# A two-layer state-space mix: preparing the per-kernel numbers once, in three widths, and a new order of the queues

## The chip, the cores and the metric

The program runs on one core of a Trainium2 chip. The metric is the device time of one execution in microseconds, given as the median of several executions. A core has a tensor engine (PE, whose weight loads are listed as PEld), a vector engine (DVE), a scalar engine for tables of functions (ACT), a general engine (POOL) and SP, which here only starts DMA transfers. Each engine works through its own queue in order and waits on semaphores for what others have to deliver.

## The reference

Two S4 layers with different parameters read the same input u (2048 steps, 512 channels). Each layer builds one long convolution kernel per channel from 128 complex modes, convolves and adds a skip; a gate mixes the two results.

```python
def layer(u, A_re, A_im, B_re, B_im, C_re, C_im, log_dt, Dskip):
    dt = jnp.exp(log_dt)[:, None]
    logdA = dt * (A_re + 1j * A_im)                     # 512 x 128
    dB = dt * (B_re + 1j * B_im)
    P = jnp.exp(logdA[:, :, None] * arange(L))          # 512 x 128 x 2048
    K = jnp.einsum("dn,dnl,dn->dl", C_re + 1j * C_im, P, dB).real
    y = irfft(rfft(pad(u)) * rfft(pad(K)))[:L]          # causal convolution
    return y + u * Dskip

g = sigmoid((u * gate_w).sum(-1, keepdims=True))
return g * layer_A(u) + (1 - g) * layer_B(u)
```

## The kernel before

The 512 channels are cut into 8 chunks of 64; a chunk has 128 kernels (64 channels of both layers), one row of 128 numbers per parameter and mode. All arithmetic is float32, with angles as 32-bit integers that wrap. The work of a chunk has these parts:

- **Preparation** (`prep`, `N` = 128 columns): from the parameter rows and dt 35 small instructions make five numbers per kernel and mode: `al` (decay times dt), `rho` (size of C times B times dt), and the integer angles `z64`, `wa`, `zh`. Five products are fixed on POOL and one on DVE, twelve more may go to either (`heng="any"`); the others are DVE operations, a reciprocal (line 432) among them, and five functions on ACT. Results and temporaries lie in rings of tiles of one chunk's width (`par_in`, `m1`, `m2`, `m`, `e`, `kr`, `al`, `rho`, `z64`, `wa`, `zh`), most with one buffer. dt is spread over the partitions once (`spread_dt`), stored in DRAM (`dtd`) and read back for each chunk (`load_dt`).
- **Seeds** (`seed`, `seed_angles`): 25 exponentials on ACT in a row (line 471) write powers of the decay into `ml` and `mh`; three POOL products write angles `sa` and multiply `rho` into `mh`.
- **Tables** (`tables`, eight per chunk, T = 0 to 63, 16 kernels each): POOL forms the angles `ang`; POOL or DVE forms the decays `mr` from `ml` (128x1024) and from `mh` (128x512); ACT makes sine, half-angle sine and square into PSUM (`s`, `sq`); four DVE operations (lines 514 to 519, shown as L297 and L307) multiply them into `ei` and `mr`, of which the last two are the L307 instructions that write `mr`. PE (line 529) sums over the modes into the kernel's samples, which ACT or DVE copies to `kt`; after every second table PE runs the first stage of the kernel's Fourier transform (`first`, L549) into `xa` or `xb`.
- **Convolution** (`conv`, eight steps per chunk, s = 0 to 63): PE finishes the transform (L631, `fw`), DVE multiplies with the spectrum of u (L635, `y`), PE runs the first inverse stage with the constants `vv` (L644, L645), a copy to `z` and a store to `zb` follow.
- **End** (`fin`): `zb` is read back as `f`, PE runs the last inverse stage with the gate matrix `gsi` (L673), and the result is stored.

Beside them `u_spectra` makes the spectra of u (L549, L572), which go to DRAM, and `gated` makes the gate matrix (L593). The constants `w2` and `vv` are loaded at the start.

`prep(n)` for the next chunk stands in the program at the first table of a chunk, so the preparation of chunks 1 to 7 is spread over the whole run. What is executed when is not the program's order: `ORDER`, a list of 2068 numbers, gives the order of all operations, and so each queue's; a `b` behind a number takes the second of two possible engines (DVE instead of POOL for products, DVE instead of ACT for copies). Helpers record the operations, so many have the same line in the profile: L297 is `tensor_tensor`, L302 `tensor_scalar`, L307 `scalar_tensor_tensor`, L310 ACT functions, L320 and L322 copies on ACT and DVE, L315 transfers.

Of the kernel before, what the change touches and what calls it, by code (L numbers as in the profile page):

```python
# [22 lines left out]
CH = 2 * DC  # L23
# [4 lines left out]
GROUPS = tuple((c,) for c in range(8))  # L28
# [50 lines left out]
1 0 3 89 93 250 23 24 25 249 26 27 28 41b 44b 30 31 46b 43 5 47 90 42 9 45 32 48 55 33 54 49 34 35 6 7 22 92 91b 97 50 2 51 94  # L79
17 14 29 52b 36 4 53 37 82 12 38 15 95b 13 39 64 101 56 65 96 66 20 57 98 58b 71b 61 67b 62b 68 59 63 40 70 75 60 251 76 100b  # L80
69 72 73 77 74b 79 99b 253 309 102 252b 254 16 8 322 83 103 104b 310 111 78 114 313 311b 324b 312b 84 85 325b 316 340 86 314
87 317 112 115b 275 315 113 123 323 129 116 318 80 326 120 338 319 327 329 81 124 117 339 328 125 330 133 341b 342 331 351 320
343 352 332 121 353b 118 333 321 119 344 122 345 255 278 277 276 280b 346 10 354 355 11 279 367 281 356 334b 347 348 335 88
257 256 358 368 357 349 369 359 282 336 360 371 105 382 361 106 350 258 107 337 370b 372 362 380 374 18 1501 373 108 381 375
363 126 383b 384 376 109 385 110 130 377 396 398 127 387 386 259 397 388 131 283 400 1494 389 409 1487 1495 401 399 390 137
1488 132 284 1502 290 402 364 285 128 261 260 291 286b 292b 378 287 289 298 293 295 365 288 274 296b 366b 466 299 425 379b 134
305b 304b 297 300 403 410 391 141 19 426 136b 21 135b 404 138 405 294 301b 392b 306 139 411b 413 393 302 307 412b 308b 406 303
429 140 428 416 394 395 427 142 417 414 468b 415 407 430 467 144 418 143 469 470 419 479 471 420 473 480 472 474 481 483 475
151 408 421b 484 431 476 482 422 152 495 486 153 496 487 148 423 497b 424 145 149 485 435 477 150 146b 499 498b 147 154 488
510 500 157 478b 489 155 1489 432 156 501 508 160 1490 158 490 524 159 502 262 433 1496 509 491 503 161 1491 162 437 504 512  # L90
511 1497 526 166 1492 515 513 163 1493 527 167 1503 516 168 505 492 434 1504 525 514 436 164 517 1510 1508 537 439 1509 493
165 528 506 494b 538 1515 518 529 1498 169 1516 539 531 1522 530 532 507b 519 553 1499 1511 541 1500 1505 554 533 1529 542 540
520b 1512 534 555 1506 544 543 1530 521 545 1523 1507 1513 447 556 546 557 1514 1517 558 448 535 566 1518 522 523 449b 1524
1536 536b 438 452 547 568 560 548 559 263 440 453b 450 561 567 1525 569 570 454 562 623 441 571 583 549b 264 442 265 573 1519
574 563 1531 1526 445 1520 270 572 1532 271 1527 443 582 1528 1538 451 1543 266 550 272 1521 1537 1550 575 1544 267 273 1551
564 551b 576 268 577 446 552 625b 1533 638b 565 444 578 269b 456 579 1539 462 455 1534 1535 461 580 463b 1557 457 581 464 1558
458b 465b 1545 459 654b 586 1540 585 1546 636 460 1571 1552 1572 1541 1547 584 1553 624 1542 1564 1559 1565 1548 626 627 1554
1560 1549 637 628 630 655 1578 1566 629 589 631 1561 1947 590 592 1567 591 640 639 1555 632 1573 1562 1556 594 1568 587 593
633 1579 652 596 1574 595 1563 1943 641 653 634 643 1585 642 1948 1586 644 1569 1592 602 665 645 1570 1575 635 1949 1950 666
656 646 647 657 603 598b 597 659 667 658 1944 660 1576 1580 683 661 648 1945 1946 669 649 1939 1581 1577 668 670 1606 173 662  # L100
1587 671 650 684 672 1935 1593 663 681 1582 682 1588 664 694 673 599 1599 1594 1600 604 651 685 605 688 674 600 1940 696 601
1583 1584 170 613 612 1941 686 1936 619b 614 606b 181 689 615 171 695 675 172 1937 174 609 687 1595 697 676 607 176 1607 177
690 710 698 711 175 691 677 699 678 610b 701 712 700 1589 702 680 679 723 703 714 692 724 704 1590 611 705 713b 715 1591 618b
1613 740 717 693 716 178 1614 718 706 1596 719 727 725 180 179b 728 720 707 729 620b 1597b 621 588 616 708 739 709b 182 622b
726b 721 780 209 1598 184b 743 730 608 617 183b 741 731 185 191 732 781 793 733 722 192b 186 794 734 784 193 782b 1942 188 187
1963 742 735 785 736 783b 795 189 787 190 197 737 1959 786 788 200 749b 738 796b 198 1601 789 811 199 1964 201 790 797 202 809
# [5 lines left out]
1655 754 886 763b 1656 766 764 745 1649 1961 865b 866 1638 1662 767b 896 768 887 937 888 1645 897 765 756 889 1650 878 890 950  # L112
1639b 760 755 1651 1640 891 757 1646 758 939b 1669 1652 1663 759 952b 769 892 1670 1647 1962 770 879 775b 1653 893 776b 777b
1654 771 778 772b 1952 779b 773 895 894b 899 900 1657 774 898 1956 1658 938 1953b 1664 1683 906b 941 1684 1979 1971 1659 940b
953b 942 968 903 1665 904 943 944 1671 1676 1957 1660 1666 1958 945 1677 908 1672 946 1661 951 1980 1954 901 947 954 969 966
948 1975 955 967 905 957 1678 956 958 1667 979 1981 959 970 1982 980 213 1673 1972 973 1690 981 1691 909 971 1679 1973 1974
907 960 1685 982 910 974 1674 949 918 972 961 917 1686 912 983 1976 911 975 1697 997 962 1967 1668 963 976 1977 1698 984 986
1675 1704 995 1705 985 916 919 977 1692 913 964 1008 978 987 1680 914 920b 915 988 996 965 1968 998 999 989 1693 1009 990 1681
1000 926 1682 1010 1002 1687 927 1969 991 1003 1001 933b 902 1699 921 928 923 1012 1011b 992 1688 1004 922 1024 1689 1694 1711
993 1005 929 994 1025 1700 1013 1006 932 1015 1695 1026 1014 1696 1706 1712 1016 1007 1701 1017 1028 934 924 1029 935 930 1018  # L120
1027 210 1702 1707 931 1030 1037 217 1031 211 1038 212 214 1032 925 1039b 1019 1041 221 1718 215 1040 1033 1725 1719 1020 1708
# [82 lines left out]
def ssm_mix(ctx: ExitStack, tc: tile.TileContext, a, out, dry=False):  # L204
# [180 lines left out]
    def prep(c, heng="any"):  # L385
# [18 lines left out]
        def W(n):  # L404
            return K(n)[:1]
# [360 lines left out]
```

## Time and profile before

| | before |
|---|---|
| median of 3 runs (lowest to highest) | 526.46 us (526.21 to 527.22) |
| the profiled execution, its span | 522.11 us, 520.3 us |
| mean granted PE clock | 0.950 |
| HBM read, written | 51.25 MB, 29.82 MB |

The profile is of one execution. Its page gives busy time by engine, a strip of 40 slices, the DMA queues, the chain of work that ended last, and groups of instructions as "line engine operation out<-in, shapes, count, busy us, mean ns of one, idle time before". Other views answer for a stretch of time, a tile or a wait. An instruction's duration includes time in which it stood at a resource that another engine held, and DVE's and ACT's instructions overlap a little with the next one of their queue.

### The profile page before, as it was taken

Reading aid. Unit: us, or ns where it says so; the run is one execution under the profiler, and the core shown is the slowest. Engines: PE = TensorE matmul, PEld = TensorE weight load, DVE = VectorE, ACT = ScalarE, POOL = GpSimd, SP = SyncE. Lnnn points to the kernel's source line nnn. Section 1 sums busy time; section 2 is a strip of 40 time slices with the busy share of each in tenths; the row PEclk is TensorE's granted clock in tenths of the full one; section 3 lists DMA queues with packets and bytes.
Section 4 is the critical chain, followed back from the end, with each engine's and each line's share of the span. In section 5 each row is a group of like instructions: output and inputs, shape, how many; then the busy total and the mean of one; then the engine's idle time right before and its main releaser. Section 6 shows DMA issues by size and latency. Waiting matters only on the chain.

```text
span 520.3 us, 24035 instructions
## 1 busy us (share of the span) xinstructions
PE 427.2 (82%) x10566; PEld 396.2 (76%) x10566; DVE 442.9 (85%) x585; ACT 386.5 (74%) x694; POOL 371.7 (71%) x352
## 2 busy tenths in 40 slices
PE   3949868888699776998789879799798779799964
PEld 3738757887698766988688868699787669699964
DVE  6798989999879999999699989999899979795520
ACT  3976998677867889999668888879977697792110
POOL 2797778895498778897488986797988589770000
PEclk9987979999999999999899997989999798999997
DMA  7954571560467535563485343455557466554476
GB/s 225 313 162 132 177 245 64 153 186 10 130 183 224 156 103 153 166 183 115 134 243 164 90 151 106 132 144 153 159 160 206 117 173 195 138 154 114 156 218 164
DMA packets 82520, 82.62 MB, mean 159 GB/s; under 512 B 5904, under 2 KB 68880, under 8 KB 82416
## 3 DMA queue, kind: packets, MB, share of 16 engines
q1 hardware_dynamic: 82272, 80.69, 52.2%
q8 instruction: 83, 1.36, 1.1%
q0 software_dynamic: 144, 0.39, 0.2%
q14 instruction: 21, 0.17, 0.1%
HBM read 51.25 MB, written 29.82 MB: 156 GB/s over the span
## 4 chain that ended last, share of the span: by engine, by line
PE 35%; DVE 22%; ACT 20%; issue 9%; DMA 8%; POOL 3%; SPq 2%; DVEq 0%; ACTq 0%; POOLq 0%
PE c L644 6%; PE fw L631 6%; PE c L645 6%; PE c L529 5%; DVE mr L307 5%; PE c L549 5%; DVE ei L297 4%; DVE mr L297 4%; ACT ml L471 3%; DVE y L635 3%; ACT mh L471 3%; PE c L673 3%; DMA f<-zb 2%; DMA u<-us 2%; ACT sq L310 2%
## 5 line engine op out<-in xcount | busy, mean ns | idle before, releaser
L307 DVE SCALAR_TENSOR_TENSOR mr<-sq,mr 128x1024 f32<-128x1024 f32 (+1 forms) x128 | 118.4, 947 | 7.0 <-ACT sq L310 7.0
L644 PE MATMUL c<-y,vv 128*128 128x128 f32 x512 | 104.0, 285 | 5.9 <-ACT z L320 2.6
L297 POOL TENSOR_TENSOR mr<-ml 128x1024 f32<-128x1024 f32 x47 | 94.3, 2006 | 11.6 <-PE c L529 8.3
L645 PE MATMUL c<-y,vv 128*128 128x128 f32 x512 | 100.9, 279 | 1.2 <-issue 1.2
L297 POOL TENSOR_TENSOR ang<-zh,cint 128x512 int32<-128x512 int32 x64 | 69.2, 1082 | 28.2 <-ACT sq L310 22.5
L644 PEld LDWEIGHTS c<-y,vv 128*128 128x128 f32 x512 | 79.6, 196 | 8.6 <-ACT z L320 2.8
L529 PE MATMUL c<-mr 128*32 128x64 f32 x2048 | 67.9, 229 | 16.7 <-DVE mr L307 8.3
L310 ACT ACTIVATE s<-ang 128x1024 f32<-128x1024 int32 x64 | 66.0, 1031 | 20.0 <-DVE ei L307 10.9
L635 DVE TENSOR_TENSOR y<-fw,u 128x1024 f32<-128x1024 f32 x57 | 69.4, 1217 | 13.4 <-PE fw L631 11.8
L297 DVE TENSOR_TENSOR ei<-s,mr 128x1024 f32<-128x1024 f32 x64 | 77.7, 1215 | 3.4 <-ACT s L310 1.6
L645 PEld LDWEIGHTS c<-y,vv 128*128 128x128 f32 x512 | 79.6, 196 | 0.8 <-issue 0.8
L320 ACT ACTIVATE z<-c 128x512 f32<-128x512 f32 x84 | 49.1, 590 | 41.0 <-PE c L645 35.8
L310 ACT ACTIVATE sq<-ang 128x1024 f32<-128x1024 f32 x64 | 65.8, 1029 | 17.6 <-DVE mr L307 16.7
L297 POOL TENSOR_TENSOR ang<-sa 128x512 int32<-128x512 int32 x64 | 70.7, 1105 | 0.4
L529 PE MATMUL c<-ei 128*32 128x64 f32 x2048 | 66.9, 226 | 2.3 <-issue 2.3
L529 PEld LDWEIGHTS c<-mr 128*32 128x32 f32 x2048 | 50.3, 114 | 24.0 <-issue 8.8
L310 ACT ACTIVATE ang<-ang 128x1024 f32<-128x1024 int32 x64 | 67.6, 1056 | 1.1
L529 PEld LDWEIGHTS c<-ei 128*32 128x32 f32 x2048 | 52.4, 115 | 2.6 <-issue 2.6
L297 POOL TENSOR_TENSOR mr<-mh 128x512 f32<-128x512 f32 x45 | 51.5, 1146 | 0.0
L549 PE MATMUL c<-small,kt 64*64 64x64 f32 x2048 | 43.0, 229 | 10.1 <-ACT kt L320 5.3
L549 PEld LDWEIGHTS c<-small,kt 64*64 64x64 f32 x2048 | 37.1, 141 | 15.5 <-ACT kt L320 6.2
L307 DVE SCALAR_TENSOR_TENSOR ei<-s,mr 128x512 f32<-128x512 f32 x64 | 43.4, 679 | 0.0
(104 smaller groups left out, 828.8 us busy)
## 6 DMA issues: line engine op xcount, KB each, us to landing
zb<-z SPq DMA_DIRECT2D x64, 256.0 KB, 3.0
u<-us SPq DMA_DIRECT2D x114, 128.0 KB, 3.6
f<-zb SPq DMA_DIRECT2D x28, 512.0 KB, 5.5
us<-z SPq DMA_DIRECT2D x32, 256.0 KB, 2.5
uin<-in_uk_dram SPq DMA_DIRECT2D x16, 256.0 KB, 4.3
f<-in_ut_dram SPq DMA_DIRECT2D x8, 512.0 KB, 5.3
out_dram<-o SPq DMA_DIRECT2D x29, 128.0 KB, 3.6
par_in<-in_par_dram SPq DMA_DIRECT2D x8, 384.0 KB, 3.5
```

The costliest lines, as they stand in the source:

```text
L297: op(engs, 0, lambda e: (dve if e == "dve" else pool).tensor_tensor(out=out(), in0=in0(), in1=in1(), op=o), reads, writes, port=port)
L307: lambda _: dve.scalar_tensor_tensor(out=out(), in0=in0(), scalar=s, in1=in1(), op0=o0, op1=o1), reads, writes, port=port)
L310: op("act", c_act(n), lambda _: act.activation(out=out(), in_=in_(), func=func, **{k: v() if callable(v) else v for k, v in kw.items()}), ...
L320: act.activation(out=o(), in_=i(), func=AF.Copy)
L471: act.activation(out=t(*tile)[:, ks, j], in_=t("al", n)[:, w, ks], func=AF.Exp, scale=float(l))
L529: pe.matmul(ps[32 * j:32 * j + 32, o, 0:64], x[:, 4 * o + j, 64:96], x[:, 4 * o + j, 0:64], start=o + part == 0, stop=False, tile_position ...
L549: pe.matmul(t(*ps[h]).rearrange("p a b -> p (a b)")[64 * r:64 * r + 64, 64 * g:64 * g + 64], t(*x)[64 * h:64 * h + 64, g], t("small")[64 * ...
L631: pe.matmul(fv()[:, :, k], t("w2", j // 2)[:, 4 * (j % 2) + k], t(*x1)[:, 4 * j + k], start=True, stop=True)
L635: op("dve", 1134, lambda _: dve.tensor_tensor(out=t(*y).rearrange("p h s f d -> p h s (f d)"), in0=fv().rearrange("p s f d -> p s (f d)"). ...
L644: pe.matmul(t(*ps)[:, k], v[:, 64:192], t(*y)[:, 0, :, k], start=True, stop=False)
L645: pe.matmul(t(*ps)[:, k], v[:, 0:128], t(*y)[:, 1, :, k], start=False, stop=True)
L673: pe.matmul(t(*ps)[64 * r:64 * r + 64, i, 0:DC], t("gsi")[:, 4 * k + i, s, 64 * r:64 * r + 64], fv()[:, r, i, DC * s:DC * s + DC], start=s ...
```

## The change

The chunks are prepared in three groups: chunk 0 alone, chunks 1 to 3 together (384 columns) and chunks 4 to 7 together (512 columns), all in the head. `INS` (the six parameter rows and dt) of the two wide groups lie in the tile of `gsi`, and the temporaries in the four tiles of `vv`; both get their own contents afterwards, so the four `vv` loads and the gate copies stand behind the preparation. Chunk 0's rows lie in two `y` tiles. The five results of a wide group are stored to a DRAM tensor `prd` by five transfers; `load_par` reads one chunk's five rows (320 KB) into a ring `par` of two buffers, one chunk ahead. dt is no longer stored and read back.

The products of the wide groups stand for DVE first (`yna`), with `b` now naming POOL. No form of arithmetic changes. The order list is new throughout, 1901 numbers long. Counted from it:

| engine, operation | before | after |
|---|---|---|
| DVE instructions | 585 | 518 |
| DVE preparation | 152 | 76 (26 for chunk 0, 25 for each wide group) |
| POOL preparation | 88 | 14 |
| ACT preparation | 40 | 15 |
| `mr` products from `ml` on DVE, POOL | 17, 47 | 4, 60 |
| `mr` products from `mh` on DVE, POOL | 19, 45 | 7, 57 |
| `z`, `xa`, `xb` copies of 512 on ACT, DVE | 155, 37 | 129, 63 |
| `kt`, `o` copies of 256 on ACT, DVE | 78, 18 | 70, 26 |
| PE matrix products | the same | the same |

Up to table 4's last DVE operation the new order has all 50 DVE operations of the wide groups, 10 of their POOL operations, and three instead of two of the gate's row products. Behind it, DVE has 129 preparation operations fewer, 26 `mr` products become 7 (2 of 128x1024, 5 of 128x512, from 14 and 14 behind table 4), and copies to `z`, `xa`, `xb` on DVE rise from 31 to 54.

```diff
-GROUPS = tuple((c,) for c in range(8))
+GROUPS = ((0,), (1, 2, 3), (4, 5, 6, 7))
...
-    ring("par_in", 1, [128, GW, 7, CH])
-    for n in ("m1", "m2", "m", "e", "kr", "al", "rho"):
-        ring(n, 1, [128, GW, CH])
-    for n in ("z64", "wa"):
-        ring(n, 1, [128, GW, CH], I32)
-    ring("zh", 2, [128, GW, CH], I32)
+    ring("par", 2, [128, 5, CH], I32)
...
-        tiles["dtd",] = dp.tile([NCH, 128, CH], F32, name="dtd")
+        tiles["prd",] = dp.tile([NCH, 128, 5, CH], I32, name="prd")
...
     def load_params(n):
         for i, c in enumerate(GROUPS[n]):
...
+            if n:
+                dma(1100, lambda i=i: t("gsi").rearrange("p i s m -> p (i s m)").rearrange("p (r c k) -> p r c k", r=8, k=CH)[:, 0:6, i],
+                    lambda c=c: a["par"][c], (), [("row", r) for r in INS])
...
+    def load_par(c):
+        n = [c in g for g in GROUPS].index(True)
+        dma(350, lambda: t("par", c), lambda: t("prd")[c], [("prd", n, r) for r in OUTS], [("par", c)])
...
+    def place(n, name):
+        if n == 0:
...
+        w = CH * len(GROUPS[n])
+        if name in TEMPS:
+            k, i = divmod(TEMPS.index(name), 3)
+            return lambda: t("vv", k).rearrange("p f m -> p (f m)")[:, 512 * i:512 * i + w], w, ("row", name), []
+        i = 5 + n if name == "dt" else INS.index(name)
+        return lambda: t("gsi").rearrange("p i s m -> p (i s m)")[:, 512 * i:512 * i + w], w, \
...
+        def mul(o, x, y, kind=OP.mult):
+            r = rd(o, x, y)
+            tt("any" if n == 0 else "yna", N, V(o), V(x), V(y), kind, r, W(o), 2)
...
+        if n:
+            c0, w = GROUPS[n][0], len(GROUPS[n])
+            for i, r in enumerate(OUTS):
+                dma(90 * w, lambda i=i: t("prd")[c0:c0 + w, :, i].rearrange("c p k -> p c k"),
+                    lambda r=r: V(r, I32)().rearrange("p (c k) -> p c k", k=CH), K(r), [("prd", n, r)])
...
-    load_dt(1)
+    for n in (1, 2):
+        load_params(n)
+        prep(n)
+    for k in range(4):
+        load_w("vv", k, 192)
...
-            if c + 1 < NCH and where[c + 1][1] == 0:
-                n = where[c + 1][0]
-                if c:
-                    load_params(n)
-                    load_dt(n)
-                prep(n)
+            if c + 1 < NCH:
+                load_par(c + 1)
```

More of the change, by code (lines that the diff above doesn't have):

```diff
@@ L214, in ssm_mix @@
     NT = NCH * NG
-    GW = max(len(g) for g in GROUPS)
-    where = {c: (n, i) for n, cs in enumerate(GROUPS) for i, c in enumerate(cs)}
     NJ = F1 // 4
@@ L370, in spread_dt @@
            [("small",), ("dt",)], [key])
-        for h in range(0, n, 4):
-            m = min(4, n - h)
-            ps = ("c", "spread", lo, h)
+        for g, cs in enumerate(GROUPS):
+            if (g == 0) != (lo == 0):
+                continue
+            h, m, ps = cs[0] - lo, len(cs), ("c", "spread", g)
             op("pe", 214 * m, lambda _, h=h, m=m, ps=ps: pe.matmul(t(*ps)[:, 0:m], t("small")[:, 449:577], dg()[:, h:h + m],
-                                                                  start=True, stop=True), [key, ("small",)], [ps])
-            if lo == 0:
-                actv(CH, lambda: t("par_in", 0)[:, 0, 6], lambda ps=ps: t(*ps)[:, 0], AF.Copy, [ps, ("par_in", 0)], [("dt", 0)])
-            else:
-                actv(CH * m, lambda h=h, m=m: dg()[:, h:h + m], lambda ps=ps, m=m: t(*ps)[:, 0:m], AF.Copy,
-                     [ps], [key])
@@ L381, in spread_dt @@
-        if lo:
-            dma(1300, lambda: t("dtd")[lo:lo + n].rearrange("c p k -> p c k"), dg, [key], [("dtd",)])
-    def prep(c, heng="any"):
-        w = len(GROUPS[c])
-        N = w * CH
-        rows = ("a_re", "a_im", "c_re", "b_re", "c_im", "b_im", "dt")
-        px = ("par_in", c)
-        def V(n, d=None):
-            if n in rows:
-                v = lambda: t(*px)[:, 0:w, rows.index(n)]
-            else:
-                v = lambda: t(n, c)[:, 0:w]
+                                                              start=True, stop=True), [key, ("small",)], [ps])
@@ L397, in V, with prep @@
+    def prep(n):
+        N = place(n, "dt")[1]
+        new = set()
+        def V(name, d=None):
+            v = place(n, name)[0]
             return v if d is None else lambda: v().bitcast(d)
         def K(*names):
-            keys = [("dt", c) if n == "dt" else ("row", n, c) if n in rows else (n, c) for n in names]
-            return keys + [px] * any(n in rows for n in names)
-        quarter = lambda: t("small")[:, 577:578]
-        def W(n):
-            return K(n)[:1]
-        def mul(eng, o, x, y, kind=OP.mult):
-            tt(eng, N, V(o), V(x), V(y), kind, K(x, y, o) if o in rows else K(x, y), W(o), 2)
@@ L423, in prep, with W, rd @@
-        mul(heng, "m1", "c_re", "b_re")
-        mul("pool", "b_im", "b_im", "c_im", OP.add)
-        mul(heng, "m1", "m1", "m2", OP.subtract)
+            return [k for x in names for k in (place(n, x)[2], *place(n, x)[3])]
+        def W(name):
+            _, _, key, tile_ = place(n, name)
+            first = [k for k in tile_ if k not in new and k != ("y", "prep", 0)]
+            new.update(first)
+            return [key] + first
+        def rd(o, *names):
+            return K(*names) + [k for k in place(n, o)[3] if k in new or k == ("y", "prep", 0)]
@@ L430, in prep @@
         t2(s, ap, 1e-30, aq, OP.max, OP.add)
-        mul(heng, d, aq, ap, OP.subtract)
+        mul(d, aq, ap, OP.subtract)
         op("dve", 67 + 6.27 * N, lambda _: dve.reciprocal(out=V(s)(), in_=V(s)()), K(s), W(s))
-        mul(heng, d, d, s)
+        mul(d, d, s)
         f(d, d, AF.Arctan, table=9)
@@ L596, in gated @@
             op("pe", 3440, mm, [*fs, ("gate_w",)], [ps], table="full")
-            copy(512, lambda h=h: t("gsi")[:, 4 * h:4 * h + 4, 0], lambda ps=ps: t(*ps), [ps], [w])
+            copy(512, lambda h=h: t("gsi")[:, 4 * h:4 * h + 4, 0], lambda ps=ps: t(*ps), [ps],
+                 [w] + [("row", r) for r in INS] + [("row", "dt", n) for n in (1, 2)])
         ws = [("gsi", h) for h in range(4)]
@@ L691, in ssm_mix @@
         load_w("w2", k, 128)
-    load_params(1)
     load("dsk")
-    for k in range(4):
-        load_w("vv", k, 192)
     actv(1, lambda: t("dummy"), lambda: t("dummy"), AF.Exp, [("dummy",)], [("dummy",)], table=0)
```

205 lines of the change are left out of this document (105 added, 100 removed), and 35 rows, old and new, of the table ORDER.

## The prediction

> **What bounds the kernel now.** I read the page first: busy times and the chain that ended last.
>
> ```profile
> span 520.3 us, 24035 instructions
> ...
> PE 427.2 (82%) x10566; PEld 396.2 (76%) x10566; DVE 442.9 (85%) x585; ACT 386.5 (74%) x694; POOL 371.7 (71%) x352
> ...
> PE 35%; DVE 22%; ACT 20%; issue 9%; DMA 8%; POOL 3%; SPq 2%; DVEq 0%; ACTq 0%; POOLq 0%
> ```
>
> Nobody is full over the span: PE 82%, DVE 85%, ACT 74%, POOL 72%. The chain walks over PE, DVE and ACT in turn, so the kernel is a pipeline in which several engines are nearly full at once, and an average share decides nothing. I therefore cut the span at two places that mean the same in both orders. The instructions of line 307 that write mr come two to a table (128x1024, then 128x512); the tenth on DVE closes table 4 and ends at 55.7:
>
> ```profile
> 53.91 1.81 DVE L307 SCALAR_TENSOR_TENSOR mr<-sq,mr 128x1024 f32<-128x1024 f32 x2
> ```
>
> The other cut is 457, where table 60 is closed. The windows view over these stretches (busy us of each engine, with instruction counts):
>
> ```profile
> core 0: us, PE busy (x) PEld busy (x) DVE busy (x) ACT busy (x) POOL busy (x), PEclk, DMA share, GB/s
> 0.00:56.00 56.00, 38.74 (x740) 32.44 (x744) 44.79 (x76) 39.16 (x73) 38.25 (x48) 0.91 0.67 213
> 56.00:457.00 401.00, 337.52 (x8877) 314.66 (x8867) 369.11 (x478) 329.05 (x593) 323.48 (x296) 0.96 0.51 151
> 457.00:520.30 63.30, 50.97 (x967) 49.07 (x965) 29.02 (x33) 18.29 (x30) 9.93 (x10) 0.94 0.58 163
> ```
>
> The head is 56 us: DVE 80%, PE 69%. The middle is 401 us: DVE 92%, PE 84.2%, ACT 82%, POOL 81%. The tail has no per-kernel numbers in it and POOL nearly idle. So DVE leads the middle, but there is a second resource that DVE and POOL hold in common. The timeline by engine at 300 us:
>
> ```profile
> 299.38 3.67 POOL L297 TENSOR_TENSOR sa<-z,cint 128x1536 int32<-128x1536 int32 x1 [0.23 <-DVE z L302]
> 301.43 1.78 DVE L297 TENSOR_TENSOR rho<-rho,par_in 128x128 f32<-128x128 f32 x1
> ```
>
> A DVE product of 128 elements takes 1.78 us; it ends at 303.21, just behind POOL's 3.67 us one, which ends at 303.05. The same group by duration (min/median/max, ns) and a larger one:
>
> ```profile
> L297 DVE TENSOR_TENSOR rho<-rho,par_in x8: 281/418/2135, 19.3 to 423.5; 128x128 f32<-128x128 f32 x8
> ```
>
> ```profile
> L297 DVE TENSOR_TENSOR mr<-mh x19: 677/1293/2446, 26.9 to 428.5; 128x512 f32<-128x512 f32 x19
> ```
>
> The same instruction costs 281 or 2135 ns, 677 or 2446 ns. That is waiting on POOL, counted as DVE's busy time. The Trainium skill, "SBUF — State Buffer", section "SBUF: two separate sides", says that DVE and GpSimd share one pair of ports under an exclusive lock which the first to start keeps for its whole instruction; the two rows at 300 us agree.
>
> **The change part by part.** Counts are read off the two order lists, split at table 4 and priced by rows of before.
>
> *Wide preparation, into the head.* All seven later chunks are now prepared ahead of table 4, as groups of 384 and 512 elements. Per group DVE gets 17 two-input operations, 7 one-input ones and a reciprocal. Rows for the price:
>
> ```profile
> L297 DVE TENSOR_TENSOR ei<-s,mr 128x1024 f32<-128x1024 f32 x64 | 77.7, 1215 | 3.4 <-ACT s L310 1.6 <-PE c L533 1.0
> L307 DVE SCALAR_TENSOR_TENSOR ei<-s,mr 128x512 f32<-128x512 f32 x64 | 43.4, 679 | 0.0
> L432 DVE RECIPROCAL par_in<-par_in 128x128 f32<-128x128 f32 x8 | 7.5, 941 | 0.0
> L302 DVE TENSOR_SCALAR m<-par_in 128x128 int32<-128x128 f32 x8 | 1.8, 219 | 0.0
> ```
>
> Two-input: (1215−679)/512 = 1.047 ns an element, 143 fixed, so 545 ns for 384 and 679 for 512. One-input: (219−143)/128 = 0.59, so 371 and 447. Reciprocal: (941−143)/128 = 6.23, so 2.54 and 3.34 us. Group one: 17×0.545+7×0.371+2.54 = 14.4; group two: 17×0.679+7×0.447+3.34 = 18.0; together 32.4 us of DVE, if nothing holds the port. Also in the head DVE gains four chunk-0 products (4×0.281 = 1.1), three copies and two short dt copies (about 3.1) and loses four mr products and two small ones (−6.4). Sum: +30.2 us.
>
> *Moved work.* The new order gives most mr products to POOL and copies to DVE:
>
> ```profile
> L297 POOL TENSOR_TENSOR mr<-ml 128x1024 f32<-128x1024 f32 x47 | 94.3, 2006 | 11.6 <-PE c L529 8.3 <-issue 2.2 <-ACT ml L471 1.2
> L297 POOL TENSOR_TENSOR mr<-mh 128x512 f32<-128x512 f32 x45 | 51.5, 1146 | 0.0
> L297 DVE TENSOR_TENSOR mr<-mh 128x512 f32<-128x512 f32 x19 | 25.5, 1348 | 0.0
> L297 DVE TENSOR_TENSOR mr<-ml 128x1024 f32<-128x1024 f32 x17 | 23.6, 1400 | 4.3 <-ACT ml L471 4.3
> L320 ACT ACTIVATE z<-c 128x512 f32<-128x512 f32 x84 | 49.1, 590 | 41.0 <-PE c L645 35.8 <-DMA us<-z 1.9 <-PE c L572 1.0
> L320 ACT ACTIVATE xb<-c 128x512 f32<-128x512 f32 x45 | 27.3, 633 | 7.1 <-PE c L549 7.1
> L322 DVE COPY xb<-c 128x512 f32<-128x512 f32 x19 | 12.9, 686 | 6.8 <-PE c L549 6.8
> L593 PE MATMUL c<-f,gate_w 128*128 128x256 f32 x64 | 19.8, 478 | 0.8 <-ACT xb L320 0.5 <-ACT z L320 0.3
> ```
>
> *Preparation, out of the middle.* What goes there, by the windows view of tiles par_in (DVE, ACT, POOL) and kr (DVE, POOL), and groups that these miss:
>
> ```profile
> 56.00:457.00 401.00, 39.77 (x84) 9.18 (x27) 25.03 (x51) 0.96 0.51 151
> ```
>
> ```profile
> 56.00:457.00 401.00, 12.69 (x30) 2.38 (x5) 0.96 0.51 151
> ```
>
> ```profile
> L302 DVE TENSOR_SCALAR e<-m 128x128 f32<-128x128 f32 x8 | 5.3, 668 | 0.0
> L297 POOL TENSOR_TENSOR wa<-wa,m 128x128 int32<-128x128 int32 x8 | 4.2, 526 | 9.3 <-DVE m L302 9.3
> L297 POOL TENSOR_TENSOR wa<-zh,cint 128x128 int32<-128x128 int32 x8 | 3.8, 469 | 2.3 <-DVE zh L302 2.3
> ```
>
> Middle, engine by engine. DVE: −39.8−12.7−7×0.668 = −57.2 of preparation; 12 fewer 128x1024 and 9 fewer 128x512 mr products, −12×1.400−9×1.348 = −28.9; 23 more copies, +23×0.686 = +15.8; seven smaller copies, under 4.8. 369 becomes about 301. POOL: −25.0−2.4−7×(0.526+0.469) = −34.4, and +12×2.006+9×1.146 = +34.4: it stays at 323. ACT: −9.2, −14×0.590−11×0.633: 329 becomes about 305. PE: one row product of four goes to the head, −19.8/4: 332.5. So the middle turns from a stretch led by DVE into one led by PE.
>
> *What the head costs.* Table 4 waits behind the 30.2 us if DVE is full from there on. Port sum up to table 4: POOL 38.3 plus ten wide operations (about 10), plus 5.4 of mr, less nine small ones (−4.7), is 49; DVE's port operations (wide without reciprocals 26.5, chunk 0 about 7, mr 5.5, the dt arithmetic about 3) are 42; 91 us against 56, that is +35 with no gap. Lower end: the 11.2 us that DVE idles in the head take in part of it, +19. Upper end: each of 48 port operations waits as the e<-m row does on average (668 against 219 for a like operation), 48×0.45 = 21.6 more, +52. I take +33, between the two near sums, since both resources have that work in either order.
>
> *What the middle gives.* It needs 332.5 us of PE. At the share of today, 84.2%, it would take 395 (−6). To see what share is reachable:
>
> ```profile
> 217.00:241.00 24.00, 22.14 (x617) 20.51 (x616) 23.14 (x32) 22.32 (x34) 21.53 (x20) 1.00 0.53 155
> 340.00:360.00 20.00, 20.00 (x503) 19.06 (x502) 18.75 (x28) 16.62 (x27) 17.02 (x20) 0.95 0.51 141
> 120.00:140.00 20.00, 15.24 (x350) 14.09 (x349) 17.14 (x24) 18.95 (x43) 10.21 (x10) 1.00 0.22 61
> 400.00:420.00 20.00, 14.81 (x356) 13.98 (x346) 19.38 (x27) 14.55 (x22) 11.77 (x15) 0.83 0.49 146
> ```
>
> At 217 to 241 PE runs at 92% with DVE at 96%; at 340 to 360 at 100%. At 120 and at 400 it falls to 76% and 74%; the first holds a block of seeding exponentials on ACT, the second much preparation, with DVE at 97%. Seeds stay, preparation goes, and DVE's load falls to about 301/361 = 83%. I take the 92% of the well-fed stretch: 361.4 us, −39.6. The ends are 84.2% and 97%: −6 and −58. Break-even with a head of +33 is 332.5/368 = 90.4%.
>
> *Transfers and queues.*
>
> ```profile
> us<-z SPq DMA_DIRECT2D x32, 256.0 KB, 2.5
> par_in<-in_par_dram SPq DMA_DIRECT2D x8, 384.0 KB, 3.5
> vv<-in_vv_dram SPq DMA_DIRECT2D x4, 768.0 KB, 7.9
> ```
>
> Ten writes of the prepared numbers (192 or 256 KB) and seven loads of 320 KB come in, one write and seven short loads go: about 2.5 us and under 3.5 us each, a chunk ahead of their use, so priced at nothing; without that cover a chunk's first seed would wait 3.5 us, seven times. The writes stand in SP's queue between stores and loads of the u spectra and wait there for preparation; what is late then is a z buffer for a copy, a few us, inside the head's ends. The constants vv now load behind the preparation, since its temporaries lie in their tiles: 7.9 us to landing, ahead of the first inverse product, which stands behind table 8; if it were late, 7.9 us once.
>
> Sum: +33 −39.6 + 0 (tail) = −6.6 on the profiled execution's span of 520.3, so 513.7. That execution took 522.11 against the median 526.46; I carry the difference over: 526.46 − 6.6 = 519.9.
>
> **The rivals.**
>
> *The middle does not tighten (slower).* PE's gaps are made by ACT's seed blocks and by copies waiting for PE, both of which stay, and POOL still has 323 us. For it: 120 to 140 is at 76% with DVE at only 86%. Against it: DVE at 97% around 400. It decides from a share under 90.4%; at 87% the middle takes 382.2, −18.8 + 33 = +14.2: 540.7.
>
> *The port bounds the head (slower).* The wide operations meet POOL's as the narrow ones did: +52, with a middle of −39.6, is +12.4: 538.9. It decides from a head over +39.6. Against it: in the new order DVE runs almost all of group two with four POOL instructions between. By the skill's page on SBUF, each collision costs the loser the winner's whole remainder, so a single badly placed product would pay up to POOL's 3.67 us; this rival is that rule at work.
>
> *PE is fed throughout (faster).* Share 95%: 350.0, −51.0 + 33 = −18.0: 508.5. For it: 340 to 360. Against it: 120 to 140, with its seed block, is far from it, and every chunk has one. The granted clock was 0.83 at 400 to 420 and 1.00 at 217 to 241. The skill's "TensorE: Matmul & The Clock Gate", part 1, holds that idle windows halve the clock and busy ones restore it; the second row agrees, 120 to 140 (76%, clock 1.00) does not show it, so it changes no number here.
>
> *The change only shifts (same).* Head and middle cancel, share at 90 to 91%: within 0.2%, 526.
>
> **How the numbers follow.** Forecast, share 90.5 to 94% and head 28 to 38: 0.41; middle not tightening 0.28; port in the head 0.11; fed throughout 0.20. A measurement of this kernel tells about 0.2% (1.05 us) from no change. Of the forecast's 0.41, 0.32 lies below 525.4, 0.06 within 1.05 of 526.46, 0.03 above; with the rivals' edges: faster 0.52, same 0.07, slower 0.41. The forecast's own range is 511 to 528. Over all cases 504 to 541: a share of 97% with a head of +33 would give 501 and lies just outside, both slow rivals lie inside.
>
> **What would show it.** In the trace of after: table 4's last DVE operation at 89 (86 to 95 is right, over 96 the port rival, under 80 the lower end); wide two-input operations at 545 and 679 ns (over 1 us: the port); DVE about 301 and PE about 332 busy between tables 4 and 60, that stretch 361 us long; small durations of e, rho and kr gone from the middle; mr on POOL 60 and 57 times. Wrong would be a PE share under 90% with DVE near 80%: then ACT's seeds or POOL, not DVE, set the middle.

## The result, and the profile after

The changed kernel takes 510.78 us (507.48 to 514.88, median of 4 runs) against 526.82 (526.21 to 527.22) beside it: a ratio of 0.97, 95% interval 0.962 to 0.978. The forecast was 519.9 in a range of 504 to 541, so the sign and the range held; a gain of 6.6 us was forecast and 16 were measured. The profiled execution of the changed kernel took 514.88 us with a span of 513.1, against 522.11 and 520.3 before.

Busy times and the chain that ended last, from the page of the changed kernel:

```profile
span 513.1 us, 23881 instructions
...
PE 419.7 (82%) x10566; PEld 392.4 (76%) x10566; DVE 407.1 (79%) x518; ACT 363.8 (71%) x632; POOL 374.3 (73%) x305
...
PE 57%; DMA 11%; DVE 8%; ACT 7%; issue 7%; POOL 6%; SPq 1%; ACTq 0%; DVEq 0%; POOLq 0%
```

In the chain PE's share rose from 35% to 57% and DVE's and ACT's fell from 22% and 20% to 8% and 7%. VectorE lost 36 us of busy time (442.9 to 407.1), ACT 23, and PE, which does the same work, 7.5.

The cuts of the prediction lie elsewhere now. Table 4 is closed by the second of these two instructions, table 60 by the second row (in the timeline of DVE):

```profile
80.52 1.81 DVE L293 SCALAR_TENSOR_TENSOR mr<-sq,mr 128x1024 f32<-128x1024 f32 x2
...
449.46 0.68 DVE L293 SCALAR_TENSOR_TENSOR mr<-sq,mr 128x512 f32<-128x512 f32 x1
```

So table 4 closes at 82.3 (55.7 before) and table 60 at 450.1 (457.4). The windows over these stretches, after:

```profile
core 0: us, PE busy (x) PEld busy (x) DVE busy (x) ACT busy (x) POOL busy (x), PEclk, DMA share, GB/s
0.00:82.30 82.30, 41.76 (x782) 35.62 (x783) 70.19 (x129) 42.90 (x78) 47.96 (x50) 0.75 0.58 181
82.30:450.00 367.70, 326.27 (x8824) 306.76 (x8823) 307.95 (x358) 302.93 (x527) 315.61 (x246) 0.97 0.57 166
450.00:513.10 63.10, 51.65 (x965) 50.02 (x963) 28.96 (x33) 17.97 (x30) 10.73 (x11) 0.92 0.57 164
```

The head grew by 26.6 us, the middle shrank from 401.7 to 367.8, that is by 33.9, and the tail stayed at 63 (62.9 before): −7.3 at table 60, −7.2 at the end.

To see where in the middle it came from I closed tables 8 and 16 in the same way, in every kernel run. Times are in us; each column is the time between two closings, "after again" is the changed kernel profiled a second time. The ratios below leave out executions more than 1.5% above the fastest of their kernel, and the "after again" row is from one of those:

| kernel | to table 4 | 4 to 8 | 8 to 16 | 16 to 60 | rest | span |
|---|---|---|---|---|---|---|
| before | 55.7 | 29.5 | 69.6 | 302.7 | 62.9 | 520.3 |
| after | 82.3 | 30.9 | 54.2 | 282.8 | 63.0 | 513.1 |
| after again | 81.0 | 31.5 | 54.0 | 285.5 | 63.8 | 515.7 |
| narrow preparation | 73.4 | 30.3 | 54.6 | 279.8 | 62.5 | 500.5 |
| before, no later preparation | 56.1 | 28.3 | 67.7 | 286.7 | 62.7 | 501.4 |
| before, mr products moved | 54.2 | 29.2 | 71.2 | 309.6 | 65.0 | 529.1 |
| after, mr products back | 82.6 | 31.6 | 59.9 | 289.6 | 63.3 | 527.0 |
| after, copies back | 81.0 | 37.1 | 56.3 | 294.9 | 64.0 | 533.3 |
| after, both back | 82.8 | 36.4 | 61.1 | 294.0 | 63.3 | 537.7 |
| after, short seeds | 81.1 | 30.7 | 54.3 | 280.4 | 62.4 | 508.9 |
| after, copies back, short seeds | 84.1 | 37.4 | 54.6 | 281.6 | 64.3 | 522.1 |
| after, u spectra early | 87.9 | 33.3 | 53.4 | 283.7 | 63.5 | 521.9 |
| after, late constants | 81.0 | 30.3 | 53.2 | 289.1 | 63.6 | 517.1 |
| after, late constants and row write | 84.1 | 30.9 | 52.6 | 281.1 | 63.3 | 512.1 |

At table 16 the change is 12.7 us behind (167.4 against 154.7): the stretch from 8 to 16 already gives 15.4 back. Over the 44 tables from 16 to 60 it gains 19.9, or 0.45 us a table.

Each row is one execution. Behind table 16 six of these kernels run the same operations in the same order (after, after again, narrow preparation, u spectra early and the two with late constants), and they need 279.8 to 289.1 us there. So a difference of under some 9 us between two rows of that column shows nothing by itself. In the two columns ahead of it after, after again and narrow preparation differ by about 1 us.

### The profile page after: what moved, and what is told of

It reads as the page before. It is cut to its first block, busy times and chain, and to the rows that moved or that the text cites. A ratio compares the mean times of both kernels' runs of the same rounds, so it can differ in the third digit from the quotient of the medians.

```text
span 513.1 us, 23881 instructions
## 1 busy us (share of the span) xinstructions
PE 419.7 (82%) x10566; PEld 392.4 (76%) x10566; DVE 407.1 (79%) x518; ACT 363.8 (71%) x632; POOL 374.3 (73%) x305
## 4 chain that ended last, share of the span: by engine, by line
PE 57%; DMA 11%; DVE 8%; ACT 7%; issue 7%; POOL 6%; SPq 1%; ACTq 0%; DVEq 0%; POOLq 0%
PE c L665 11%; PE c L549 10%; PE fw L652 10%; PE c L666 10%; PE c L569 8%; PE c L694 4%; DMA f<-zb 3%; POOL mr L283 3%; PE c L592 3%; DMA zb<-z 2%; POOL ang L283 2%; DMA u<-us 2%; DVE gsi L283 2%; SPq L301 1%; DMA gsi<-in_par_dram 1%
## 5 line engine op out<-in xcount | busy, mean ns | idle before, releaser
L283 POOL TENSOR_TENSOR mr<-ml 128x1024 f32<-128x1024 f32 x60 | 119.1, 1985 | 19.3 <-issue 6.6
L283 POOL TENSOR_TENSOR ang<-par,cint 128x512 int32<-128x512 int32 x64 | 68.6, 1072 | 27.8 <-ACT sq L296 23.8
L549 PE MATMUL c<-mr 128*32 128x64 f32 x2048 | 69.2, 230 | 17.0 <-DVE mr L293 10.4
L665 PEld LDWEIGHTS c<-y,vv 128*128 128x128 f32 x512 | 78.5, 194 | 5.1 <-issue 2.9
L666 PEld LDWEIGHTS c<-y,vv 128*128 128x128 f32 x512 | 78.9, 194 | 1.1 <-issue 1.1
L296 ACT ACTIVATE s<-ang 128x1024 f32<-128x1024 int32 x64 | 66.0, 1031 | 15.7 <-DVE ei L293 12.9
L306 ACT ACTIVATE z<-c 128x512 f32<-128x512 f32 x70 | 41.3, 596 | 46.2 <-PE c L666 29.6
L549 PE MATMUL c<-ei 128*32 128x64 f32 x2048 | 68.3, 228 | 3.7 <-issue 3.7
L549 PEld LDWEIGHTS c<-mr 128*32 128x32 f32 x2048 | 50.3, 115 | 26.2 <-issue 15.4
L283 POOL TENSOR_TENSOR mr<-mh 128x512 f32<-128x512 f32 x57 | 60.9, 1069 | 0.2
L569 PE MATMUL c<-small,kt 64*64 64x64 f32 x2048 | 39.2, 222 | 6.3 <-issue 4.6
L592 PE MATMUL c<-xb,w 128*128 128x128 f32 x256 | 38.2, 300 | 5.5 <-DVE xb L308 3.6
```

The lines of the kernel that those rows point to most:

```text
L283: op(engs, 0, lambda e: (dve if e == "dve" else pool).tensor_tensor(out=out(), in0=in0(), in1=in1(), op=o), reads, writes, port=port)
L296: op("act", c_act(n), lambda _: act.activation(out=out(), in_=in_(), func=func, **{k: v() if callable(v) else v for k, v in kw.items()}), ...
L306: act.activation(out=o(), in_=i(), func=AF.Copy)
L549: pe.matmul(ps[32 * j:32 * j + 32, o, 0:64], x[:, 4 * o + j, 64:96], x[:, 4 * o + j, 0:64], start=o + part == 0, stop=False, tile_position ...
L569: pe.matmul(t(*ps[h]).rearrange("p a b -> p (a b)")[64 * r:64 * r + 64, 64 * g:64 * g + 64], t(*x)[64 * h:64 * h + 64, g], t("small")[64 * ...
L592: pe.matmul(p[:, k], t("w2", j // 2)[:, 4 * (j % 2) + k], t(*x1)[:, 4 * j + k], start=True, stop=True)
```

## The experiments

The first four ran on one chip (the kernel before: 524.29 us), the next four on a second (524.12), the last four on a third (530.0). Times are compared as ratios to the kernel before on the same chip, each with its interval; the changed kernel's own are 0.970 (0.962 to 0.978) and, run again on the second chip, 0.976 (0.966 to 0.985).

**Narrow preparation.** The wide groups are computed at 128 columns; one chunk's numbers are written for all chunks of the group.

```diff
-        w = CH * len(GROUPS[n])
+        w = CH
...
-                    lambda r=r: V(r, I32)().rearrange("p (c k) -> p c k", k=CH), K(r), [("prd", n, r)])
+                    lambda r=r: V(r, I32)().unsqueeze(1).to_broadcast([128, w, CH]), K(r), [("prd", n, r)])
```

> The changed kernel, with the wide preparation done for 128 columns instead of 384 and 512 (each chunk of a group then gets the numbers of the group's first chunk; the transfers stay as large). The 50 DVE operations of the two groups fall from 32.4 to about 14.4 us, so 18 us of DVE leave the head. If the head's length is DVE's work and PE is the bound behind it (the prediction's reading), table 4 closes about 18 us earlier and the time falls by 13 to 18 us, to about 495. If the head is held by the transfers of the second group's rows and by PE's low clock instead, table 4 moves by under 8 us and the time by under 6.

Measured: 505.81 us, ratio 0.966 (0.956 to 0.976); by time it can't be told from the changed kernel. The trace says more: table 2 closes at 58.2 instead of 73.5, table 4 at 73.4 instead of 82.3. Of the 15.3 us by which DVE is earlier 6.4 go at once, between tables 2 and 4:

```profile
58.20:73.40 15.20, 13.81 (x247) 11.79 (x248) 8.24 (x11) 8.27 (x11) 10.82 (x10) 0.78 0.57 166
```

PE is busy there for 13.8 of 15.2 us at a mean clock of 0.78: it runs a gate row (6.69 us; such a row took 3.72 at 80.65 in the changed kernel) and more behind it, which the wide preparation had covered. So in these two profiles the width costs 9 us, which are still there at table 16 (158.3 against 167.4). That is less than I expected: the head isn't DVE's alone once DVE is lighter.

**Before, without the later preparation.** The preparation of chunks 2 to 7 is left out of the kernel before, so those chunks run on chunk 1's numbers.

```diff
+                lo = len(op.ops)
                 prep(n)
+                if n > 1:
+                    left_out.update(range(lo, len(op.ops)))
```

> The kernel before, with the preparation of chunks 2 to 7 left out (their seeds and tables read chunk 1's numbers; the loads stay, the order of all else too). In the middle 50 us of DVE, 32 of POOL and 9 of ACT go. If preparation in the middle is what held it (the prediction's reading of the gain), the time falls by 20 to 35 us, to 492 to 507. If the gain behind table 4 came from the moved mr products and copies and from the new order, and preparation was cover, it falls by under 10 us.

Measured: 502.66 us, ratio 0.957 (0.949 to 0.964). The row of the table shows where: 16.0 us between tables 16 and 60, 1.9 between 8 and 16. The six preparations, 42 us of DVE's busy time between tables 4 and 60 (369.8 to 328.0), were worth some 20 us of time. They explain most of what the change gains behind table 16 (16.0 of 19.9), and nearly nothing of what it gains between 8 and 16. There it is partly work that the new order does earlier, and partly the moved work (next). PE's busy time in that stretch, before and after:

```profile
85.20:154.70 69.50, 59.35 (x1188) 56.34 (x1187) 61.63 (x80) 51.07 (x89) 52.39 (x54) 0.98 0.44 131
```

```profile
113.20:167.40 54.20, 50.79 (x1128) 47.83 (x1127) 49.47 (x58) 46.82 (x78) 51.34 (x40) 1.00 0.58 167
```

**Before, mr products moved, and after, mr products back.** The 25 products that write mr and stand on DVE in the one and on POOL in the other kernel (table 5 on) change sides; nothing else moves. (Behind table 4 DVE has 28 such products before the change, 14 of each width, and 7 after it.)

```diff
 ORDER (25 such words)     before            after
-                          383b              433
+                          383               433b
```

> The kernel before with 25 mr products behind table 4 (12 of 128x1024, 13 of 128x512) done by POOL instead of DVE, at the same places of the order: the same products that the change moves. DVE loses about 34 us, POOL gains about 39. If the move alone carries the gain, the time falls by 8 to 20 us. If it only pays once POOL is rid of its preparation (the prediction's: POOL's load stays level, since 34 us leave it), POOL goes over 90% of the middle and the time rises by 3 to 20 us.

> The changed kernel with those 25 mr products back on DVE, at the same places of the order. DVE gains about 34 us in the middle (to 93% of it), POOL loses 39. If PE is the bound of the middle and DVE has room (84%), the time rises by under 8 us; if the move to POOL is what made the middle shorter, it rises by 10 to 25 us; if POOL and not PE is the bound there now, it falls.

Measured: 527.08, ratio 1.010 (1.005 to 1.015), and 524.92, ratio 1.003 (0.998 to 1.008). With the preparation still in the middle the move loses 1%, as expected, though POOL is busy for 85% of the stretch from table 4 to table 60 and not for over 90%. With the preparation gone, putting the products back costs 3.3% by the ratios, some 17 us, and 13.9 us of span against the changed kernel's first profile: 5.7 between tables 8 and 16, and 6.8 from 16 to 60, which is within the scatter of that column.

**After again.**

> The changed kernel once more, unedited, beside the next three on the same chip. Its first profile had clock 0.926 and a span of 513.1; the other runs of it were 507.5 and 508.9 at 0.953, 512.7 at 0.928. Theory: the time of an execution goes with its granted clock, so fast runs lie between 506 and 514 and those with the higher clock are the shorter ones. Rival: clock and time are unrelated, and runs at one clock differ as much as runs at two.

Measured: 517.43 us at clock 0.940, 507.62 at 0.941, 513.27 at 0.950, 515.99 at 0.946. Two executions at one clock differ by 10 us: the rival holds. What makes the scatter of about 2% between executions of the changed kernel is not shown as a whole. Between tables 16 and 60 two terms of it can be seen in the six kernels named above: PE is busy for 250 to 258 us with the same 6973 matmuls, at clocks of 0.98 down to 0.95, and stands idle without a named releaser ("issue") for 13 to 19 us.

**After, u spectra early.**

```diff
 ORDER, behind the first transform of table 1's pair
-... 335 387 ... 339 ... 399 ... 192 ... 210 ... 214 ...
+... 387 386 ... 192 ... 210 ... 214 ... 222 ... 218 ... 226 229 232 235 238 241 244 ... 399 ... 335 ... 339 ...
```

> The changed kernel with TensorE's work of the u spectra of chunks 2 and 3 (four first transforms and six of the eight products) taken forward into the time in which VectorE prepares group two and TensorE stood idle (it waited 13.7 us there for one load), their copies on ScalarE; the gate rows that stood there go behind the preparation. TensorE gets 12 x 1.16 us of work ahead of table 4 in that place and gives 3 x 3.72 us back to later. Theory (VectorE sets the head, TensorE the middle): table 4 stays within 2 us of 82, the stretch from table 4 to table 60 loses about as much as TensorE's busy time in it falls, so 4 to 9 us shorter than the changed kernel. Rival (the middle is set by the hand-overs between VectorE, ScalarE and GpSimd): within 2 us of the changed kernel.

Measured: 525.58, ratio 1.001 (0.996 to 1.006): 11 us slower than the changed kernel instead of 4 to 9 faster. ACT's timeline shows the place (the bracket names the idle time and what ended it):

```profile
72.01 0.60 ACT L318 ACTIVATE z<-c 128x512 f32<-128x512 f32 x1 [0.59 <-DMA us<-z]
73.68 0.60 ACT L318 ACTIVATE z<-c 128x512 f32<-128x512 f32 x1 [1.08 <-DMA us<-z]
74.85 0.60 ACT L318 ACTIVATE z<-c 128x512 f32<-128x512 f32 x1 [0.57 <-DMA us<-z]
77.85 0.60 ACT L318 ACTIVATE z<-c 128x512 f32<-128x512 f32 x1 [2.41 <-DMA us<-z]
78.35 1.02 ACT L308 ACTIVATE s<-ang 128x1024 f32<-128x1024 int32 x1
```

A copy to `z` needs one of two buffers, and these wait for their stores to DRAM. ACT stood in its queue behind them, and table 3's sine came 6 us late; table 4 closes at 87.9. That spoils the test up to table 8. Behind it nothing moved: 53.4 and 283.7 against 54.2 and 282.8. But PE's busy time hardly fell there either (50.3 us against 50.8 between tables 8 and 16), so this run does not decide between theory and rival.

**After, short seeds.** Five of the 25 exponentials of each seeding block are kept in chunks 2 to 7; the other columns keep what an earlier chunk left.

```diff
-                for tile, j, l in cols:
+                for tile, j, l in cols if c < 2 else cols[::5]:
```

> The changed kernel with 5 instead of 25 exponentials in each seeding block of chunks 2 to 7 (the other columns keep what an earlier chunk left there), which takes 6 x 20 x 0.24 = 29 us of ScalarE's busy time out of the middle. Theory (TensorE sets the middle): under 6 us faster than the changed kernel. Rival, named in the prediction for a TensorE share under 90% (ScalarE's seeding blocks set the middle): 15 to 29 us faster.

Measured: 511.52, ratio 0.978 (0.971 to 0.985) against 0.976 for the changed kernel on that chip: the theory holds. Between tables 16 and 60 ACT's busy time fell from 231 to 210 us; the stretch, 280.4, can't be told from the changed kernel's.

**After, copies back, alone and with short seeds.** The PSUM copies behind table 4 go back to the engines that the kernel before gave them; then also with the edit above.

```diff
 ORDER (49 words lose their b, 18 gain it)
-411b
+411
```

> The changed kernel with the PSUM copies behind table 4 on the engines that the kernel before gave them (49 go from VectorE to ScalarE, 18 the other way; about 16 us net), the products that write mr staying on GpSimd. Theory (with the preparation gone VectorE has room, TensorE leads): within 4 us of the changed kernel, since ScalarE has as little room as VectorE, and the 14 us that the mr products cost when put back came from VectorE being full again. Rival (the spread of the copies is itself a good part of the gain): 5 to 15 us slower than the changed kernel.

> The changed kernel with the copies back on the engines of before and, at once, 5 instead of 25 exponentials in each seeding block of chunks 2 to 7 (the other columns keep what an earlier chunk left). The copies alone cost 12 us between tables 16 and 60 (294.9 against 282.8), the short seeds alone saved 2.4. Theory (copies on ScalarE stand behind its seeding blocks of 6 us, and TensorE behind the copies): with short blocks that stretch falls to 282 to 286. Rival (the cost is something else, such as where each copy stands in its engine's order): 291 to 295.

Measured: 532.91, ratio 1.019 (1.014 to 1.024), beyond even the rival; with short seeds 520.62, ratio 0.984 (0.974 to 0.994). DVE's busy time between tables 16 and 60 fell to 223 us of 295 and still everything was slower:

```profile
167.40:450.10 282.70, 253.90 (x6973) 239.60 (x6972) 236.95 (x274) 231.39 (x401) 238.75 (x187) 0.96 0.58 168
```

```profile
174.40:469.30 294.90, 256.57 (x6973) 242.13 (x6972) 223.35 (x250) 241.78 (x426) 239.87 (x187) 0.96 0.56 161
```

```profile
176.20:457.80 281.60, 252.35 (x6973) 237.73 (x6972) 225.99 (x249) 219.16 (x326) 238.54 (x187) 0.98 0.59 169
```

The three rows are the stretch from 16 to 60 of after, of the copies back, and of the copies back with short seeds. With short seeds it is as short as in the changed kernel (281.6). By the ratios short seeds give 3.5% with the copies on ACT (1.019 to 0.984) and nothing without (0.976 and 0.978). So the copies cost time because of ACT's seeds. My reading is that a copy that stands behind a block of exponentials on ACT keeps PE waiting, and that taking either the copies or the block away removes that. The short seeds also take 23 us of load off ACT, and the runs do not separate the two. The stretch from 4 to 8 stays at 37 in both; the block that runs in it is chunk 1's, which was not shortened. The wait can be watched there, in the timelines of ACT and of PE with the copies back:

```profile
99.75 2.66 ACT L501 ACTIVATE mh<-par 128x128 f32<-128x128 f32 x11
102.22 3.21 ACT L501 ACTIVATE ml<-par 128x128 f32<-128x128 f32 x14
105.23 1.12 ACT L318 ACTIVATE xa<-c 128x512 f32<-128x512 f32 x2
```

```profile
105.91 2.48 PE L581 MATMUL c<-small,uin 64*64 64x64 f32 x64 [6.02 <-ACT xa L318]
```

The exponentials run from 99.75 to 105.4, the two copies to `xa` behind them, and PE starts 6.02 us late. In the changed kernel PE's longest wait for ACT in that stretch is 1.4 us. With the copies back there is one more such wait behind a block, of 3.86 us at 434.5. All of PE's waits for ACT between tables 16 and 60 add up to 9.1 us, against 6.8 in the changed kernel, so for most of the 12 us there the path is not shown.

**After, both back.** Of the change only the preparation in the head and the new order stay.

> The changed kernel with both parts of the moved work behind table 4 put back (25 mr products on VectorE and the copies as before), so that of the change only the preparation in the head and the new order stay. Put back one by one they cost 14 (products) and 18 us (copies). Theory (each part alone overloads one engine, and both together balance them again as they did before, VectorE getting the products and giving the copies): less than the sum, 15 to 22 us over the changed kernel. Rival (the costs add): 28 to 36 us over it, slower than the kernel before by 15 us or more.

Measured: 542.45, ratio 1.026 (1.017 to 1.036). Against the changed kernel's 0.970 to 0.976 on the other chips that is some 5 to 6% more, 26 to 30 us, nearer to the sum than to my theory; between tables 16 and 60 the costs do not add (294.0 against 294.9 for the copies alone), up to table 16 they do (12.9 against 6.7 and 7.0). So in this order the preparation put in the head without the moved work makes the kernel slower.

**After, late constants, and with the row write late.**

```diff
 ORDER (SP)
-... 169 ... 170 358 ... 225 ...
+... 358 169 ... 225 170 ...
 and, in the second,
-... 164 122 1321 123 203 1322 337 338 ...
+... 122 1321 123 203 1322 337 338 164 ...
```

> The changed kernel with three loads in another order on SP: the per-kernel numbers of chunk 1 ahead of the first inverse constants, and the second inverse constants (768 KB) behind the last inputs of the u spectra, some 9 us later. In the changed kernel TensorE stops for 4.5 us in the middle of a group of 64 matmuls at 88.8 us, with nothing that the profile names, while the DMA engines are 99% busy with two such loads. Theory (the instructions of TensorE come late behind these loads): that stop goes or shrinks under 1.5 us, the stretch from table 4 to table 8 is 2 to 5 us shorter than 31. Rival (the stop has another cause): stop and stretch stay.

> As the kernel with the late loads, and also the write of group two's first row is issued behind the loads of the second gate rows, which it held back until 63 us, so that TensorE waited 13.7 us for them. Theory (VectorE alone sets the head up to table 4): TensorE's wait shrinks by 4 to 9 us, table 4 stays at 81 to 83, the time is that of the kernel with the late loads within 2 us. Rival (TensorE's idle time in the head counts): 4 to 9 us faster than that.

Measured: 516.63, ratio 0.977 (0.969 to 0.984), and 512.84, ratio 0.966 (0.957 to 0.976): neither can be told from the changed kernel. PE's timeline in the changed kernel, and then with the late constants:

```profile
87.42 1.39 PE L569 MATMUL c<-small,uin 64*64 64x64 f32 x57
93.26 0.49 PE L569 MATMUL c<-small,uin 64*64 64x64 f32 x7 [4.46 <-issue]
```

```profile
86.07 1.38 PE L581 MATMUL c<-small,uin 64*64 64x64 f32 x57
88.79 0.34 PE L581 MATMUL c<-small,uin 64*64 64x64 f32 x7 [1.33 <-issue]
```

A group of 64 matmuls breaks behind its 57th in both, with no semaphore in it. The stop lies ahead of PE's 984th matmul in both, and with one 768 KB load less at that time the stop is 1.33 us instead of 4.46. The other traces bear it out: PE stops at this place for 3.2 to 4.7 us in all eight traces that have both loads there, and for 1.3 us in the two that have one of them moved. That fits instructions that come late behind transfers; which transfer carried them no row shows (the last section has more on these stops). The stretch from 4 to 8 got 0.6 us shorter, not 2 to 5, so this stop was hardly on the path. (Those 0.6 us are within the scatter, too.) The write moved behind the loads cut PE's wait for the gate's inputs from 13.7 to 8.9 us,

```profile
PE c L613 <- DMA f<-in_ut_dram: 13.7, 1, 13.7
```

```profile
PE c L625 <- DMA f<-in_ut_dram: 8.9, 1, 8.9
```

and table 4 closed 2 us later, not earlier: PE's idle time in the head is not what sets it.

## Why the prediction was right, and where it was off

**The head, +33 predicted, +26.6 measured.** The count of operations and their prices held. The groups by shape:

```profile
L283 DVE TENSOR_TENSOR vv<-gsi 128x384 f32<-128x384 f32 x3 | 1.7, 551 | 0.0
L283 DVE TENSOR_TENSOR vv<-gsi 128x512 f32<-128x512 f32 x3 | 2.0, 689 | 2.3 <-DMA gsi<-in_par_dram 2.3
L446 DVE RECIPROCAL gsi<-gsi 128x384 f32<-128x384 f32 x1 | 2.6, 2553 | 0.0
L446 DVE RECIPROCAL gsi<-gsi 128x512 f32<-128x512 f32 x1 | 3.4, 3351 | 0.0
```

545 and 679 ns had been worked out from other widths (545 to 551 and 684 to 689 here), the reciprocals 2.54 and 3.34 (2.55 and 3.35). The error is in the sum: durations were added though neighbours overlap. DVE's timeline in group two:

```profile
66.03 0.68 DVE L293 SCALAR_TENSOR_TENSOR gsi<-gsi,vv 128x512 f32<-128x512 f32 x1
66.63 0.68 DVE L283 TENSOR_TENSOR vv<-vv,vv 128x512 f32<-128x512 f32 x1
67.23 0.69 DVE L283 TENSOR_TENSOR gsi<-gsi 128x512 f32<-128x512 f32 x1
67.84 0.69 DVE L283 TENSOR_TENSOR gsi<-gsi,vv 128x512 f32<-128x512 f32 x1
```

Each starts 0.60 us behind the one before and lasts 0.69. The durations of all DVE instructions up to table 4 add up to 49.3 us before and 79.6 after, 30.3 more, as predicted (30.2). But their overlaps grew from 4.8 to 9.4 us, so DVE's busy time rose from 44.5 to 70.2, by 25.7. (The 50 wide operations alone add up to 34.8 us, 2.4 more than the 32.4 of the prediction, and the other terms came out lower by about as much.) The Trainium skill, "Perfetto Trace Analysis", section "Optimizing Scalar/DVE Operations", says this: an operation occupies DVE for its elements and about 60 ns on SBUF, and the profiled latency has about twice that overhead, because the half in which the write is acknowledged overlaps with the next. The trace agrees in kind; the overlap here is 85 to 90 ns.

The second half of that term was the port. I took +33 because the port sum said +35. The wide operations show little such waiting on DVE: the 2.4 us above their price are all that can be it, most of them in group one (one of 0.55 took 1.22 us). POOL's ten took 0.82 to 1.78 us. DVE's idle time up to table 4 was 12.1 us after and 11.2 before. So the port rival (+52) was not at work, and the port sum was no bound: POOL's 48.0 us and the 42 us counted for DVE make 90, and table 4 closed at 82.3. In group two POOL ran three operations between 50.7 and 69.6 and a fourth from 69.61 on, the four that the prediction had read from the order.

**The middle, −39.6 predicted, −33.9 measured.** VectorE fell to 308 us (301 predicted), ACT to 303 (305), POOL to 316 (323), PE to 326 (332.5). PE's share is 326.27/367.7 = 88.7%, not 92%, which is under the 90.4% named as break-even and the 90% named as wrong. (For that case the prediction named ACT's seeds or POOL. The short seeds gave nothing that can be told from the scatter. POOL, at 86%, was not tried alone; none of PE's idle time between tables 16 and 60 is put down to it.) Two pieces make it, in the windows view from table 4 to 8 and from 8 to 60, and the second piece in the kernel before:

```profile
82.30:113.20 30.90, 21.68 (x730) 19.43 (x728) 21.64 (x29) 24.82 (x49) 25.63 (x21) 0.94 0.47 150
113.20:450.10 336.90, 304.69 (x8098) 287.43 (x8097) 286.42 (x331) 278.20 (x479) 290.09 (x226) 0.97 0.58 167
```

```profile
85.20:457.40 372.20, 316.39 (x8133) 296.41 (x8132) 342.40 (x433) 300.94 (x538) 300.61 (x277) 0.96 0.52 151
```

From table 8 on the share is 304.69/336.9 = 90.4% (85.0% before, 316.39/372.2). From 4 to 8 it is 70%: there is no convolution yet to fill PE. The failed step is the choice of the best-fed 24 us of the old trace as the measure for the whole middle, start of the pipeline included: measured against 92% the start costs 7.3 us and the rest 5.7, and PE's busy time, 6.2 us under the forecast, gave some 6.8 back. So the condition of the rival "the middle does not tighten", a share under 90.4%, was met. What saved the sum is that the head's term was too large by 6.4 while the middle's was too large by 5.7; that these errors cancelled is luck.

**What gave the gain.** The prediction let the mr products and copies only change loads: DVE 301, POOL 323, ACT 305. The table says more. Preparation out of the middle is worth 16 us between tables 16 and 60 if nothing else changes, and the head takes 12.7 at table 16 even with all that comes back before it. The moved work is what makes the sum positive in this order: with both parts put back the kernel is 2.6% slower than before. For the copies the worth is not the load taken off DVE, for they put load *on* DVE; they cost time on ACT because of its seeds, and the likely way is that a copy PE waits for then stands behind 6 us of exponentials. The prediction listed the seed blocks as a reason why the middle might not tighten; by the short seeds they cost nothing measurable in the changed kernel and 3.5% with the copies on ACT. Why the mr products are better on POOL was not tested. With them back, DVE is busy for 89% of the stretch from 16 to 60 (84% in the changed kernel), and PE's waits for DVE there add up to 7.4 us instead of 3.8.

PE's idle time between tables 16 and 60, summed over pieces of at least 0.15 us by what ended them, says the same more directly. Before, it is 45.2 us: 22.4 ended by ACT, 12.2 by DVE, 3.4 by transfers and 7.2 by nothing named. Without the later preparation it is 36.3 (17.1, 5.1, 7.6 and 6.5), in the changed kernel 28.5 (6.8, 3.8, 4.8 and 13.1). The waits for ACT and DVE went; the largest part of what is left is stops for which the profile names no cause.

Two things stay open. The engines were changed back one word at a time in an order that was laid out for the others, so 14 and 18 us hold for that order, not for the assignment as such. And the new order was never run alone.

**The tail** was predicted at 0 and is +0.1. **The writes and the seven loads of 320 KB** were priced at nothing. The writes held back the gate's inputs in SP's queue and so had a part in PE's 13.7 us of waiting in the head, which the late write showed to be off the path. The one wait for a load of 320 KB was 1.4 us, on POOL.

**Profile against median.** −6.6 was made for the profiled execution and came to −7.2 there. Carried to the median it fell short: the profiled execution before was 4.3 us under its median, the one after 4.1 over. With a scatter of 2% after the change, one profile of each kernel can't carry a forecast to better than some 8 us.

## What to carry to other kernels

Put the pitch from one start to the next into a sum over one engine's queue, not the duration, and read a share that you mean to reach from the whole kind of stretch, its filling included. Before moving small work out of a full stretch, ask which instruction the leading engine waits for and which block stands ahead of it in its queue: here the place of the moved work decided the sign, and not the time freed alone. Test the parts of a change one by one and also all but one, since the part that carries the idea can lose alone.

## What the hardware showed that I had not expected

A group of matmuls without any wait stopped at the same instruction in ten traces, for 3.2 to 4.7 us beside two 768 KB loads and for 1.3 us with one of them moved away. Such stops have fixed places. PE's instructions can be counted in their order: matmuls, as many weight loads, and some 140 semaphore instructions. By this count 124 of the 127 stops of over 0.8 us that the 14 traces put down to "issue" stand at the same place of a block of 256 instructions (the 192nd or 193rd), and none of the 348 stops of that length with a named releaser does. So these stops recur at a distance of 256 instructions or a multiple of it. That fits instructions that arrive in blocks of 256 and are sometimes late, but no row shows their transfer.

TensorE's mean granted clock over a whole execution did not order the executions of one kernel: 517.43 us at 0.940 and 507.62 at 0.941.
